# Seven short rows of matmuls behind the last product

## The chip, the cores and the metric

The kernel runs on one core of one Trainium2 chip. The metric is the device time of one execution in microseconds. Beside it stands the span of a profiled execution: the time from its first to its last instruction, as the hardware profiler recorded it.

## The reference

The reference computes two residual sublayers over a sequence of 2048 rows of 512 features, all in fp32. What matters here is the shape of the work: long products, the last of them with `w_out`.

```python
mod = (_silu(c) @ w_mod).reshape(c.shape[0], 6, 1, -1)
sa, ca, ga, sb, cb, gb = (mod[:, 0], mod[:, 1], mod[:, 2], mod[:, 3], mod[:, 4], mod[:, 5])
h = _layernorm(x) * (1 + ca) + sa
a = h @ dft_hid_re.T;  b = h @ dft_hid_im.T
x = x + ga * (dft_seq_re @ a - dft_seq_im @ b)        # Fourier mixing
h = _layernorm(x) * (1 + cb) + sb
z = gelu(h @ w_in);  z1 = z[..., :Fh];  z2 = _layernorm(z[..., Fh:])
g = w_sp @ z2 + b_sp[None, :, None]                   # gating over the sequence
x = x + gb * ((z1 * g) @ w_out)                       # the last product
```

Here S is 2048, D is 512 and Fh is 896.

## The kernel before

The kernel writes each fp32 operand as a high part, rounded to the type fp32r, and a low part, the rest. A product is then three matmuls in fp32r: high by high, high by low, low by high. The helper `matmul3` (lines 94 to 98) issues them, so nearly all matmuls of the program have its lines. `split`, `prep_hi` and `prep_lo` make the parts on ScalarE (L268) and VectorE (L286).

A matmul here has a stationary operand of 128 x 128 words, loaded into the array before it, and a moving operand of 128 partitions by 512 columns. In the profile the two are separate rows: PEld LDWEIGHTS and PE MATMUL. All moving operands of the kernel lie contiguously in SBUF. A plain fp32 product occurs once, in `keep_busy` (L368), which runs four matmuls of ones at the start while the first transfers are under way. A single fp32r matmul stands at L416.

PSUM has eight banks, and the helper `bank(k, name)` takes a tile of 128 x 512 words in bank k; a new tile under the same bank number follows the previous one there. The order of all work is written out by hand: lists of things to do at step n (`at`, `run`), in the order in which the engines then execute them.

The stages in order: the Fourier products over the sequence (tiles `gp`) and over the features (`yp`), the product with `w_in` (`fp`, `z1s`, `z1p`, `z2s`, `z2p`), the gating product over the sequence (`gw`, banks 0 to 7; its last sums are taken out on VectorE by `add_w`, L952), and the last product with `w_out` (`op`). For the last one, `make_wo` and `make_wo_lo` hold the parts of `w_out` in SBUF, seven tiles `wo_hi[f]` and seven `wo_lo[f]` of 128 x 512 words, in the profile `woh` and `wol`. `mm_o` runs 7 x 3 matmuls for each of sixteen blocks of 128 rows, with the parts of `z1 * g` (`uh`, `ul`) as the stationary operand. The outputs go to banks 4 and 5 by turns; the sixteenth goes to bank 6, into which `hold_x2` (L1032) has put the residual before. `add_o` (L1019, L1020) adds the residual of the other fifteen on VectorE and sends them out.

The last block is taken out by `halves_o`: ScalarE copies its bank to SBUF (L1039), and two transfers take the two halves, one issued from ScalarE's queue (L1041) and one from SyncE's (L1042). Line 1411 stands at the very end; the program's closing drains and semaphores carry its number in the profile.

Of the kernel before, what the change touches and what calls it, by code (L numbers as in the profile page):

```python
# [8 lines left out]
F32 = mybir.dt.float32  # L9
# [4 lines left out]
P = 128  # L14
# [5 lines left out]
def fnet_gmlp_kernel(  # L20
# [32 lines left out]
    nc = tc.nc  # L53
# [3 lines left out]
    Q = 512  # L57
# [5 lines left out]
    x = x.rearrange("b s d -> (b s) d")  # L63
# [15 lines left out]
    def bank(k, name):  # L79
        return psum.tile([P, 512], F32, tag=f"bank{k}", bufs=1, name=name)  # L80
# [814 lines left out]
    wo_hi, wo_lo, wor, Z1T = {}, {}, {}, {}  # L895
# [78 lines left out]
    def make_u(p, r, f):  # L974
        g, z = G[p, r][:, f, :], Z1T[p, r]
        if f + (0 if p in (1, 4) else 4) == NF - 1:
            nc.vector.transpose(z[:, f].rearrange("p (b i) -> p b i", i=32), z[:, 3].rearrange("p (b i) -> p b i", i=32))
        nc.vector.tensor_tensor(g, g, z[:, f, :], op=ALU.mult)
# [56 lines left out]
    def halves_o(t, i):  # L1035

        ps = OP.pop((t, i))
        o = blocks.tile([P, Q], F32, tag="t", bufs=2, name="last")
        nc.scalar.activation(o, ps, AF.Copy)  # L1039
        rows_ = slice(t * Q + i * P, t * Q + (i + 1) * P)  # L1040
        nc.scalar.dma_start(out[rows_, :D // 2], o[:, :D // 2])  # L1041
        nc.sync.dma_start(out[rows_, D // 2:], o[:, D // 2:])  # L1042

    def two_first(mm, n, k, m):

        if k % m == 0:
            mm([n, n + 1])
        elif k % m > 1:
            mm([n])
# [73 lines left out]
    for j, turn, weigh, row, fold, hi in ((0, (25, 26, 27, 28), (29, 29, 30, 30), 26, (34, 34, 35, 36), (40, 37, 38, 39)),  # L1123
# [8 lines left out]
        n = weigh[3] + 1  # L1132
# [20 lines left out]
    for t in range(NQ):  # L1153
        n = 8 * NQ * (t + 1)
        for i in range(4):
            y = N2 - 1 if t == NQ - 1 else (54, 56, 58, 60)[i] if t == 0 else n + (7, 9, 11, 13)[i] if t == 1 else n + 1 + 3 * i
# [41 lines left out]
    w0 = ctx.enter_context(ExitStack())  # L1198
# [92 lines left out]
    for i, p in enumerate(PROD):  # L1291
        for k in range(8):
            n = NB[p] + 2 * k
# [11 lines left out]
    for f in range(NF):  # L1305
        n = N4 + 24 + 8 * f
# [55 lines left out]
    for o in range(len(order)):  # L1362
# [18 lines left out]
        for q in MU.get(o, ()):  # L1381
            if q[:2] == (4, 1):
                add_bs(*q)
            make_u(*q)
    halves_o(*order[-1])
    assert not fill, fill


# [27 lines left out]
```

## Time and profile before

| | us |
|---|---|
| time, median of 2 runs | 932.57 (931.79 and 933.35) |
| span of the profiled execution | 930.9 |
| time of that execution apart from its span | not recorded |
| TensorE matmuls busy | 924.6 (99% of the span) |
| weight loads busy | 760.7 (82%) |
| VectorE busy | 737.3 (79%) |
| ScalarE busy | 409.6 (44%) |
| GpSimd busy | 198.9 (21%) |

In the rows of the profile, PE is TensorE's matmuls, PEld its weight loads, DVE VectorE, ACT ScalarE, POOL GpSimd and SP SyncE; a q behind the name is the engine's queue, that is, what it issues or waits for outside its compute work. A line of the timeline has the start and the duration in microseconds, the engine, the source line, the operation, the tiles written and read, the shape and the count, and in brackets the idle time before it with what ended that. A line of a group has the count, the busy time, the mean duration in nanoseconds, and the idle time before its instructions. A line of a source view has the shortest, median and longest duration in nanoseconds and the first and last start in microseconds. A matmul's duration reaches from its start to the end of its last result, so the durations of neighbours overlap.

### The profile page before, as it was taken

What the parts mean: (1) busy time and instruction counts of PE and PEld (TensorE: products, weight loads), DVE (VectorE), ACT (ScalarE), POOL (GpSimd) and SP (SyncE); (2) the same over time, 40 slices, a digit from 0 to 9 for tenths busy, and PEclk for the clock granted to TensorE, in tenths of its full rate; (3) what the DMA queues carried; (4) which work ended last, traced back from release to release, by engine and by line L of the source; (5) the groups of instructions that cost most, each with busy time, mean ns of one, the idle gap of its engine ahead of it and who ended that gap; (6) DMA issues with size and microseconds to landing.
All of it is one profiled execution on the core that took longest, in us unless ns stands there. A gap on an engine that the chain in (4) does not pass through costs nothing.

```text
span 930.9 us, 12343 instructions
## 1 busy us (share of the span) xinstructions
PE 924.6 (99%) x4053; PEld 760.7 (82%) x4053; DVE 737.3 (79%) x1217; ACT 409.6 (44%) x734; POOL 198.9 (21%) x376
## 2 busy tenths in 40 slices
PE   8999999999999999999999999999999999999998
PEld 5888888888888888888888888888888888888886
DVE  7789967788687677875668788899799789896762
ACT  5685424232132221322577877674544544331121
POOL 2420000224654165323512320331000000000000
PEclk9999999999999999999999999999999999999999
DMA  9995762856639977996464764444464555744651
GB/s 215 219 226 123 146 158 46 192 148 163 165 86 306 306 207 222 277 337 232 138 217 135 273 204 103 118 106 104 104 147 102 132 140 138 177 102 149 188 174 57
DMA packets 246976, 157.88 MB, mean 170 GB/s; under 512 B 140384, under 2 KB 214368, under 8 KB 246784
## 3 DMA queue, kind: packets, MB, share of 16 engines
q1 hardware_dynamic: 233248, 119.57, 52.0%
q0 software_dynamic: 12272, 36.86, 11.5%
q10 hardware_dynamic: 1392, 0.66, 0.2%
q8 instruction: 32, 0.52, 0.2%
q14 instruction: 32, 0.26, 0.1%
HBM read 120.33 MB, written 36.71 MB: 169 GB/s over the span
## 4 chain that ended last, share of the span: by engine, by line
PE 98%; DMA 1%; DVE 0%; SPq 0%; issue 0%; ACTq 0%; POOL 0%; ACT 0%; DVEq 0%
PE gp L96 12%; PE gp L97 12%; PE gp L98 12%; PE gw L97 10%; PE gw L98 10%; PE gw L96 10%; PE yp L98 3%; PE yp L96 3%; PE yp L97 3%; PE op L98 3%; PE op L97 3%; PE op L96 3%; PE fp L97 1%; PE fp L98 1%; PE fp L96 1%; PE z2s L98 1%
## 5 line engine op out<-in xcount | busy, mean ns | idle before, releaser
L268 ACT ACTIVATE ah<-t 128x512 fp32r<-128x512 f32 x236 | 149.1, 632 | 364.7 <-DVE t L189 252.5
L286 DVE TENSOR_TENSOR al<-t,ah 128x512 fp32r<-128x512 f32 x236 | 160.7, 681 | 52.6 <-PE gp L97 27.9
L97 PE MATMUL gp<-al,hh 128*128 128x512 f32 x496 | 193.0, 389 | 0.0
L96 PE MATMUL gp<-ah,hh 128*128 128x512 f32 x496 | 193.0, 389 | 0.0
L98 PE MATMUL gp<-ah,hl 128*128 128x512 f32 x496 | 192.9, 389 | 0.0
L189 DVE STREAM_TRANSPOSE t<-stage 128x512 f32<-128x512 f32 x236 | 165.7, 702 | 11.2 <-DMA stage<-in_A_dft_seq_re_dram 4.9
L97 PE MATMUL gw<-al,bh 128*128 128x512 f32 x400 | 155.6, 389 | 0.0
L98 PE MATMUL gw<-ah,bl 128*128 128x512 f32 x384 | 149.5, 389 | 0.0
L96 PE MATMUL gw<-ah,bh 128*128 128x512 f32 x384 | 149.4, 389 | 0.0
L98 PEld LDWEIGHTS gp<-ah,hl 128*128 128x128 f32 x496 | 93.1, 188 | 19.4
L96 PEld LDWEIGHTS gp<-ah,hh 128*128 128x128 f32 x496 | 93.1, 188 | 19.4
L97 PEld LDWEIGHTS gp<-al,hh 128*128 128x128 f32 x496 | 93.1, 188 | 19.4 <-DVE al L286 0.2
L97 PEld LDWEIGHTS gw<-al,bh 128*128 128x128 f32 x400 | 75.1, 188 | 15.5
L98 PEld LDWEIGHTS gw<-ah,bl 128*128 128x128 f32 x384 | 72.1, 188 | 15.5 <-DVE bl L919 0.5
L96 PEld LDWEIGHTS gw<-ah,bh 128*128 128x128 f32 x384 | 72.1, 188 | 15.0
L891 POOL DMA_DIRECT2D s_d<-sj x64 | 35.1, 548 | 106.8 <-DVE sj L883 82.4
L96 PE MATMUL yp<-hth,gh 128*128 128x512 f32 x128 | 49.8, 389 | 0.0
L97 PE MATMUL yp<-htl,gh 128*128 128x512 f32 x128 | 49.8, 389 | 0.0
L98 PE MATMUL yp<-hth,gl 128*128 128x512 f32 x128 | 49.8, 389 | 0.0
L636 POOL DMA_DIRECT2D ht_d<-hturn x62 | 41.0, 667 | 23.9 <-DVE hturn L632 18.5
L96 PE MATMUL op<-woh,uh 128*128 128x512 f32 x112 | 43.6, 389 | 0.0
L97 PE MATMUL op<-wol,uh 128*128 128x512 f32 x112 | 43.6, 389 | 0.0
(233 smaller groups left out, 1446.0 us busy)
## 6 DMA issues: line engine op xcount, KB each, us to landing
stage<-in_A_dft_seq_im_dram SPq DMA_DIRECT2D x64, 256.0 KB, 5.6
sj<-in_B_w_sp_dram SPq DMA_DIRECT2D x32, 512.0 KB, 6.8
s_d<-sj POOLq DMA_DIRECT2D x64, 256.0 KB, 4.2
stage<-s_d SPq DMA_DIRECT2D x128, 128.0 KB, 2.8
stage<-in_A_dft_seq_re_dram SPq DMA_DIRECT2D x60, 256.0 KB, 5.4
stage<-in_B_w_sp_dram SPq DMA_DIRECT2D x88, 128.0 KB, 2.9
wm<-in_w_mod_dram SPq DMA_DIRECT2D x16, 256.0 KB, 6.1
xr<-in_A_x_dram POOLq DMA_DIRECT2D x16, 256.0 KB, 4.5
```

The costliest lines, as they stand in the source:

```text
L96: nc.tensor.matmul(acc, ah, bh, start=first, stop=False, skip_group_check=go_on)
L97: nc.tensor.matmul(acc, ah, bl, start=False, stop=False, skip_group_check=go_on)
L98: nc.tensor.matmul(acc, al, bh, start=False, stop=last, skip_group_check=go_on)
L189: nc.vector.transpose(dst.rearrange("p (b i) -> p b i", i=32), block[:, :, 32 * k:32 * k + 32])
L268: nc.scalar.activation(AH[n], T[n], AF.Copy)
L286: nc.vector.tensor_tensor(AL[n], t, AH[n].bitcast(F32), op=ALU.subtract)
L636: eng.dma_start(v[a, i], ht[32 * a:32 * a + 32].rearrange("c (b r) -> c b r", r=32))
L891: nc.gpsimd.dma_start(s_d[m, r, g][b * P:(b + 1) * P, :], a)
```

## The change

Behind `halves_o` of the last block the changed kernel calls a new function, `shapes`. It issues seven rows of eight matmuls. The operands are parts of `w_out`: two stationary blocks of 128 columns, `w0` and `w1`, out of `wo_hi[1]`, and two moving tiles, `a = wo_hi[0]` and `b = wo_lo[0]`, taken by turns. Each matmul starts and ends its own sum. The outputs go to new tiles in bank 0, those of the last row to banks 0 and 1 by turns, and nobody reads them. The rows:

- `sfull`: the columns as they lie.
- `sturn`: every second column, first the even and then the odd ones.
- `sline`: every sixteenth column, from sixteen starting points.
- `sparts`: two halves of 256 columns, one behind the other.
- `sone`: the first column 512 times.
- `sboth`: by turns an fp32r matmul and one whose two operands are read as plain fp32.
- `srows`: contraction over the lower and the upper 64 partitions by turns.

```diff
+    def shapes():
+
+        a, b, w = wo_hi[0], wo_lo[0], wo_hi[1]
+        w0, w1 = w[:, :P], w[:, P:2 * P]
+
+        def row(name, pairs, n=8, banks=(0,), parts=None):
+            ps = [bank(k, f"{name}{k}") for k in banks]
+            for i in range(n):
+                l, r = pairs[i % len(pairs)]
+                o = ps[i % len(ps)]
+                if parts:
+                    p0 = parts * (i % (P // parts))
+                    o = o[p0:p0 + parts]
+                if len(r.shape) == 3:
+                    o = o.rearrange("p (x y) -> p x y", y=r.shape[-1])
+                nc.tensor.matmul(o, l, r, start=True, stop=True)
+
+        def mixed(t, y):
+            return t.rearrange("p (x y) -> p y x", y=y)
+
+        row("sfull", ((w0, a), (w1, b)))
+        row("sturn", ((w0, mixed(a, 2)), (w1, mixed(b, 2))))
+        row("sline", ((w0, mixed(a, 16)), (w1, mixed(b, 16))))
+        row("sparts", ((w0, a.rearrange("p (x y) -> p x y", x=2)), (w1, b.rearrange("p (x y) -> p x y", x=2))))
+        row("sone", ((w0, a[:, :1].broadcast_to((P, Q))), (w1, b[:, :1].broadcast_to((P, Q)))))
+        row("sboth", ((w0, a), (w1.bitcast(F32), b.bitcast(F32))))
+        row("srows", ((w[:64, :P], a[:64]), (w[64:, :P], b[64:])), banks=(0, 1))
...
     halves_o(*order[-1])
+    shapes()
     assert not fill, fill
```

## The prediction

> **What bounds the kernel now.** I read the page's busy shares first, then the chain that ended last, and then, because everything in this change stands behind the last product, the last microseconds of the timeline.
>
> ```profile
> span 930.9 us, 12343 instructions
> PE 924.6 (99%) x4053; PEld 760.7 (82%) x4053; DVE 737.3 (79%) x1217; ACT 409.6 (44%) x734; POOL 198.9 (21%) x376
> PE 98%; DMA 1%; DVE 0%; SPq 0%; issue 0%; ACTq 0%; POOL 0%; ACT 0%; DVEq 0%
> L97 PE MATMUL gp<-al,hh 128*128 128x512 f32 x496 | 193.0, 389 | 0.0
> ```
>
> TensorE is the kernel: 98% of the chain, and its groups sat idle for 0.0 us. Work that is put behind it adds to the time unless something later still runs. The mean of 389 ns is not what a matmul costs, since matmuls overlap. The cost is the distance from one start to the next, and the timeline's tail gives it, together with what follows the last product:
>
> ```profile
> 914.73 0.39 PE L96 MATMUL op<-woh,uh 128*128 128x512 f32 x1
> ...
> 926.52 0.19 PEld L98 LDWEIGHTS op<-woh,ul 128*128 128x128 f32 x1
> 926.75 0.39 PE L98 MATMUL op<-woh,ul 128*128 128x512 f32 x1
> 927.17 0.60 ACT L1039 ACTIVATE last<-op 128x512 f32<-128x512 f32 x1 [8.21 <-PE op L98]
> 927.79 0.33 SPq L1042 DMA_DIRECT2D out_dram<-last  x1
> 927.80 0.38 ACTq L1041 DMA_DIRECT2D out_dram<-last  x1
> ```
>
> From the start at 914.73 to the one at 926.75 there are 53 matmuls: 12.02 / 53 = **0.227 us** each, with the 0.19 us weight load of the next one hidden under it. The last product ends at 926.75 + 0.39 = 927.14. ScalarE empties the bank until 927.77, and two transfers take the tile out. What closes the program is in the rows of its last line and in the transfers' landing times (1.7 to 2.0 us after issue):
>
> ```profile
> DMA to landing us min/median/max: 1.7/1.9/2.0
> L1411 SPq DRAIN  x3: 7/7/7, 930.0 to 930.4; - x3
> L1411 PEldq DRAIN  x2: 13/2140/4267, 922.9 to 930.4; - x2
> L1411 SPq EVENT_SEMAPHORE  x11: 17/28/28, 928.2 to 930.8; - x11
> ```
>
> The last byte lands at about 927.8 + 2.0 = 929.8. SyncE drains at 930.0, and then come 0.9 us of drains and semaphores among the engines, up to 930.9. TensorE's own first drain starts at 922.9 and takes 4.267 us, so it ends at 927.2, with the last matmul. From there TensorE is free for 930.0 - 927.1 = 2.9 us. That is all the cover there is behind the last product.
>
> The page gives the profiled execution no time beside its span of 930.9 us. The two timed runs have a median of 932.57, which is 1.7 more; I add the change of the span to 932.57.
>
> **The change part by part.** It removes nothing and moves nothing. It adds 56 matmul calls on TensorE in seven rows of eight, each 512 columns wide, over operands that have lain in SBUF since long before. No other engine gets an instruction, no queue gets a DMA, and nobody reads the results. The eviction (L1039) and the two output transfers wait on the bank of the last product alone (bank 6), so they run as before beside the rows. The rows write banks 0 and 1, whose last reader is the adding of the last sequence product:
>
> ```profile
> 891.27 2.47 DVE L952 TENSOR_TENSOR g<-gw,g 128x512 f32<-128x512 f32 x4
> ```
>
> That reader is done at 893.74, 33 us earlier, so the first row's first matmul waits for nothing and starts one distance behind the last product's: 926.75 + 0.227 = 926.98.
>
> *Plain rows.* The first row reads contiguous columns in the same kind and size as every product here: 8 x 0.227 = **1.81 us**. The row "parts" describes the same 512 contiguous columns as two halves: 1.81. The row "one" reads one column 512 times. No row of the trace has that; it costs nothing at best (1.81), and I see no reason why reading one word again should be slower than reading a new one, so I take 1.81, with 3.44 (below) as its far end.
>
> *Whole words.* The row "both" alternates four fp32r matmuls with four plain fp32 ones. The kernel has four plain fp32 calls of this size, the warming loop of line 368, and they leave eight records:
>
> ```profile
> L368 PE MATMUL busyp<-busy,ones x8: 592/1061/1193, 1.5 to 6.9; 128*128 128x512 f32 x8
> 4.23 0.34 PEld L368 LDWEIGHTS busyp<-busy,ones 128*128 128x128 f32 x1 [0.52 <-issue]
> 5.08 0.34 PEld L368 LDWEIGHTS busyp<-busy,ones 128*128 128x128 f32 x1 [0.52 <-issue]
> 6.47 1.02 PE L368 MATMUL busyp<-busy,ones 128*128 128x512 f32 x2
> ```
>
> So a plain fp32 call is two records. Early on they come 0.85 us apart (4.23 to 5.08). The last two together run from 6.47 for 1.02 us, to 7.49, and the last of them, the shortest at 0.592, began at 6.90: 0.43 us apart. The weight loads of line 368 fall from 0.34 us to 0.19 over the same stretch, the 0.19 of the tail, so at the end of the kernel the faster figure holds. A plain fp32 call costs 2 x 0.43 = 0.86 us, and the row 4 x 0.227 + 4 x 0.86 = **4.35 us**. Changing kind between neighbours is in no row; it may cost nothing, or one emptying of the array each time. What an emptied array costs can be read where TensorE waited:
>
> ```profile
> 8.74 1.20 PE L520 MATMUL gp<-al,hh 128*128 128x512 f32 x4 [0.26 <-DVE al L286]
> 807.70 0.43 PE L98 MATMUL gw<-ah,bl 128*128 128x512 f32 x1
> 807.96 0.40 PE L96 MATMUL gw<-ah,bh 128*128 128x512 f32 x1
> ```
>
> Four matmuls after a stop take 1.20 us against 3 x 0.227 + 0.389 = 1.07, so 0.13 more; with the tail of the one before (0.389 - 0.227 = 0.16) that is 0.29 us for each emptying. A wait that is met as it is asked costs 0.03 (0.26 between the starts at 807.70 and 807.96). Seven changes of kind: 0 to 2.0 us. The six changes of row, each with a new tile in the same bank, could make TensorE wait for its own writes: 0 to 6 x 0.29 = 1.7 us. I take nothing for both, since TensorE runs in order and changes its accumulation bank throughout the products with no idle time to show for it.
>
> *Strided rows.* The row "turn" reads every second word, first the even and then the odd ones (8 bytes apart); the row "line" reads every sixteenth (64 bytes apart). All products here move contiguous columns, so the trace has no row for either. The low end is 0.227 a matmul. The nearest slower rows are the plain fp32 record, 0.43, where 512 columns take two turns each, and the plain fp32 call, 0.86. For "turn", two words apart, I take the low end, 1.81. For "line", the row farthest from what the kernel does, I take the next row up: 8 x 0.43 = **3.44**; its ends are 1.81 and 8 x 0.86 = 6.88. The nearest strided reads on another engine cost nothing, but they keep 32 words together, which "line" does not:
>
> ```profile
> L189 DVE STREAM_TRANSPOSE t<-stage 128x512 f32<-128x512 f32 x236 | 165.7, 702 | 11.2 <-DMA stage<-in_A_dft_seq_re_dram 4.9
> L286 DVE TENSOR_TENSOR al<-t,ah 128x512 fp32r<-128x512 f32 x236 | 160.7, 681 | 52.6 <-PE gp L97 27.9
> ```
>
> [...]
>
> *Half rows.* The last row contracts over 64 partitions, the lower and the upper half by turns, into two banks. Every product here has 128, so bounds again: one after the other, 8 x 0.227 = 1.81; two at a time, 4 x 0.227 = 0.91. Eight weight loads of 0.188 us, should they stay one behind another, take 8 x 0.188 = **1.50**, between the two, and I take that.
>
> ```profile
> L98 PEld LDWEIGHTS op<-woh,ul x19: 187/188/188, 914.3 to 926.5; 128*128 128x128 f32 x19
> ```
>
> [...]
>
> *The sum.* 1.81 x 4 (full, turn, parts, one) + 3.44 + 4.35 + 1.50 = 16.5 us. TensorE then ends at 926.98 + 16.5 + 0.16 (the tail of the last) = 943.7. The output landed at 929.8 and no longer counts. The closing, which began at 930.0, begins when TensorE's drain ends, and its 0.9 us follow: span 944.6, 13.7 more. **932.57 + 13.7 = 946.3 us**, 1.5% slower. If the cover of 2.9 us were absent, it would be 949.2.
>
> A measurement of this kernel tells about 2% from no change: that is 18.65 us, a time of 951.2.
>
> **Rivals.**
> 1. *Order costs nothing.* All strided matmuls go at 0.227: 1.63 less, 944.6. For it: TensorE's reads are the one thing in this trace that never falters (idle 0.0 in groups of 496). Against: they are always contiguous. With the half rows in pairs too it is 944.1, the low end.
> 2. *The joints cost.* The array empties at changes of row and of kind: up to 3.7 us more, 950.0; with half of it 948.1. Against: the 0.0 us idle at bank changes in the products. For: a tile whose only accesses are TensorE's, replaced in the same bank, is met nowhere else near in time.
> 3. *Several orders cost two turns.* "turn" and "one" go at 0.43 like "line": 2 x 1.63 more, 949.6; "turn" alone 947.9.
> 4. *The other side: slower by over 2%.* fp32r keeps its single pass only for contiguous columns, and "turn" and "line" fall to the plain fp32 price of 0.86: 5.07 + 3.44 = 8.5 more, 954.8. The place is those 16 matmuls. They are in my sum with 5.25 us; it decides from 5.25 + 4.9 = 10.2 us, an average of 0.63 each, about three turns a column. For it: the plain fp32 rows prove that the same words can be read at a quarter of the pace. Against: the kind of the matmul, not its order, made that price.
> 5. *It doesn't do what it says.* Matmuls into banks nobody reads are dropped on the way to the chip, or fit into the 2.9 us of cover: 932.6. For the second the rows would have to take a fifth of the sum, which the 0.227 excludes.
>
> **How the numbers follow.** The forecast (only "line" at two turns, joints free) has 0.35; rival 1 has 0.25, rival 2 0.16, rival 3 0.08, rival 4 0.12, rival 5 0.04 (0.01 of it for a chance reading below -2%). The range runs from 943.6, a little under rival 1's low end with a closing half a microsecond shorter, to 951.0, which takes in rivals 2 and 3 and leaves out rival 4 and rival 5: 0.16 outside. Slower by over 2% is rival 4 and a little of rivals 2 and 3 together, 0.14; faster 0.01; within 2% 0.85.
>
> **What would show it.** In the changed kernel's trace all lines up to the eviction keep their times, and the matmuls of the new line start at about 927.0 with no idle time before. Read by output tile: distances of 0.227 in "full", "parts" and "one"; 0.227 in "turn" and 0.43 in "line" (0.227 there is rival 1, 0.86 in both rival 4); twelve records in "both", eight of them 0.43 apart; the half rows in 0.9 to 1.8 us. Gaps of 0.3 at the first matmul of each row or between kinds are rival 2. The transfers land near 929.8 as before, and 0.9 us lie between TensorE's end and the span's end; a wait of the closing that comes late for another reason would put the whole sum off by that much.

## The result and the profile after

The changed kernel takes **949.64 us** (949.54 and 949.74), 1.0179 times the time before, with a 95% interval of 1.0163 to 1.0196: 17.1 us more, slower, and just under the 2% that tells a change from none. The forecast was 946.3, with a range of 943.6 to 951.0. The span grew from 930.9 to 947.8.

The busy shares say only that TensorE is still the whole kernel:

```profile
span 947.8 us, 12464 instructions
PE 944.4 (100%) x4113; PEld 771.7 (81%) x4113; DVE 737.3 (78%) x1217; ACT 409.6 (43%) x734; POOL 199.1 (21%) x376
```

The chain of the changed kernel, in order of time, shows where the 17 us lie. Its columns are start, duration, and engine, tile and line; one piece is one row of eight matmuls:

```profile
926.85 0.23 PE op L98
927.07 1.83 PE sfull L1059 x8
928.90 0.04 issue
928.95 3.91 PE sturn L1059 x8
932.86 0.04 issue
932.90 3.73 PE sline L1059 x8
936.63 0.04 issue
936.67 2.12 PE sparts L1059 x8
938.79 0.04 issue
938.84 2.01 PE sone L1059 x8
940.85 0.04 issue
940.89 4.66 PE sboth L1059 x12
945.54 0.04 issue
945.59 1.20 PE srows L1059 x8
```

From the end of the last product at 927.07 to the end of the last row at 946.79 it is 19.7 us, where the prediction had 16.5 between the same two ends. Two things stand out. "turn" is as slow as "line", 3.91 against the 1.81 that it was given. And between any two rows there is a short stop. The matmuls around the first one show it:

```profile
928.27 0.39 PE L1059 MATMUL sfull<-woh,woh 128*128 128x512 f32 x1
928.50 0.39 PE L1059 MATMUL sfull<-wol,woh 128*128 128x512 f32 x1
928.95 0.71 PE L1059 MATMUL sturn<-woh,woh 128*128 128x512 f32 x1
929.48 0.64 PE L1059 MATMUL sturn<-wol,woh 128*128 128x512 f32 x1
929.94 0.64 PE L1059 MATMUL sturn<-woh,woh 128*128 128x512 f32 x1
```

The last of "full" ends at 928.50 + 0.39 = 928.89, and "turn" begins 0.06 later; in between no matmul is in flight. From 929.48 on, a matmul of "turn" comes every 0.45 us, twice the distance of a contiguous one.

The closing is as it was: drains and semaphores for 1.0 us behind TensorE's end at 946.79.

### The profile page after: what moved, and what is told of

Read it like the earlier page. It is cut to its first block, busy times and chain, and to the rows that moved or that the text cites. A ratio compares the mean times of both kernels' runs of the same rounds, so it can differ in the third digit from the quotient of the medians.

```text
span 947.8 us, 12464 instructions
## 1 busy us (share of the span) xinstructions
PE 944.4 (100%) x4113; PEld 771.7 (81%) x4113; DVE 737.3 (78%) x1217; ACT 409.6 (43%) x734; POOL 199.1 (21%) x376
## 4 chain that ended last, share of the span: by engine, by line
PE 98%; DMA 1%; DVE 0%; SPq 0%; issue 0%; ACTq 0%; POOL 0%; DVEq 0%
PE gp L98 12%; PE gp L97 12%; PE gp L96 12%; PE gw L98 10%; PE gw L96 10%; PE gw L97 10%; PE yp L98 3%; PE yp L97 3%; PE yp L96 3%; PE op L98 3%; PE op L97 3%; PE op L96 3%; PE fp L97 1%; PE fp L96 1%; PE fp L98 1%; PE z2s L96 1%
## 5 line engine op out<-in xcount | busy, mean ns | idle before, releaser
L98 PE MATMUL op<-woh,ul 128*128 128x512 f32 x112 | 43.6, 389 | 0.0
```

Source lines behind the costliest of these rows:

```text
L98: nc.tensor.matmul(acc, al, bh, start=False, stop=last, skip_group_check=go_on)
```

## The experiments

The theory after the result had two parts. A stop comes because a row's new tile waits for the last write into the tile before it in the same bank. And a strided matmul is slow because of the order of its columns. The rival of the first part was that the change of order or kind empties the array; the rival of the second, that place, bank or weight loads make those rows slow.

**The cover.** The first row is kept alone.

```diff
         row("sfull", ((w0, a), (w1, b)))
-        row("sturn", ...)   # and the five rows behind it
```

> Only the first row (eight contiguous fp32r matmuls) is left. Theory (cover): TensorE ends at 926.9 + 8 x 0.227 + 0.16 = 928.9, ahead of the last output's landing and the drain at 930.0, so nothing is added: span 930.9, time 932.6 as before. Rival (what is put behind the last product adds its length): 2.0 us more, 934.6. The difference is 0.2%, so the span and the place of the closing decide, with the time beside them.

Measured: 932.26 us, ratio 0.9999 (0.9989 to 1.0008). TensorE's last matmul ends at 930.12, and SyncE's drain comes at 931.2, after the landing of the output, which was issued at 928.97 and took up to 2.0 us:

```profile
929.73 0.39 PE L1059 MATMUL sfull<-wol,woh 128*128 128x512 f32 x1
L1434 SPq DRAIN  x3: 7/7/7, 931.2 to 931.5; - x3
```

The eight matmuls, 1.8 us behind the last product, are free. This profiled execution was already 1.2 us later when the last product began its last matmul (927.92 against 926.75), so its longer span is not theirs.

**The stops: one tile, or the same kind in new tiles, or other banks.** Three kernels. The first keeps every order and kind but one tile a bank; the second keeps the new tiles but reads everything in order; the third keeps orders, kinds and new tiles but gives neighbouring rows different banks.

```diff
-            ps = [bank(k, f"{name}{k}") for k in banks]
+            for k in banks:
+                if k not in held:
+                    held[k] = bank(k, f"s{k}")
+            ps = [held[k] for k in banks]
```

> All seven rows as in the change, but every row writes the same tile of bank 0 (and one of bank 1 for the half rows) instead of a new tile each. Theory (a new tile in the same bank makes TensorE wait for its own last write): the six joints of about 0.31 us vanish, 949.6 - 1.9 = 947.7, and the first matmul of each row follows at the distance of its row. Rival (the array empties because the order or the kind of the reading changes): joints stay, 949.6.

```diff
+        row("sfull0", ((w0, a), (w1, b)))    # and so on to sfull6
-        row("sturn", ...)
```

> Seven rows of the contiguous kind, each in a new tile of bank 0. Theory (the new tile makes the joint): six joints stay although nothing about the reading changes; TensorE takes 56 x 0.227 + 6 x 0.31 + 0.16 = 14.7 us from 926.9, span 942.6, time 944.3. Rival (the change of order makes the joint): no joints, 12.9 us, time 942.5.

```diff
-        row("sturn", ((w0, mixed(a, 2)), (w1, mixed(b, 2))))
+        row("sturn", ((w0, mixed(a, 2)), (w1, mixed(b, 2))), banks=(1,))   # then 2, 3, 7, 0, and (1, 2)
```

> The seven rows of the change, each still in a new tile, but in banks 0, 1, 2, 3, 7, 0 and 1 with 2, so that no row follows the one before it in the same bank. Theory (a new tile waits for the last write into the previous tile of its bank): that write is over by then, the six joints shrink to a wait already met, 0.03 us each; 949.6 - 1.7 = 947.9, as with one tile (947.6). Rival (any new tile, or any change of bank, empties the array): 949.6.

Measured: one tile 947.64, seven contiguous rows 944.36, banks apart 947.27, each within 0.7 us of the first theory. The chain of the kernel with the contiguous rows has a stop before each row but the first, although nothing about the reading changes. Its first two rows:

```profile
926.78 1.83 PE sfull L1059 x8
928.61 0.04 issue
928.65 2.15 PE sfull L1059 x8
```

The chain of the kernel with banks apart has none of these stops, although order and kind change at each row:

```profile
927.16 1.81 PE sfull L1059 x8
928.97 3.62 PE sturn L1059 x8
932.59 3.47 PE sline L1059 x8
936.06 1.85 PE sparts L1059 x8
937.91 1.73 PE sone L1059 x8
939.64 4.35 PE sboth L1059 x12
943.99 1.13 PE srows L1059 x8
```

The kernel with one tile a bank takes the same 17.96 us in one piece:

```profile
926.65 17.96 PE s L1063 x60
```

So neither a new tile nor a new order makes these stops. A new tile in the bank just written does. The first weight load of "turn" shows the wait: in the changed kernel it starts only behind the last matmul of "full", and with banks apart it runs under that matmul, as weight loads do within a row.

```profile
928.94 0.18 PEld L1059 LDWEIGHTS sturn<-woh,woh 128*128 128x128 f32 x1 [0.48 <-PE sfull L1059]
```

```profile
928.59 0.19 PEld L1059 LDWEIGHTS sturn<-woh,woh 128*128 128x128 f32 x1
```

The rows with banks apart also give the terms without stops: 17.96 us in all, so the six stops cost 19.72 - 17.96 = 1.8 us. Set row against row, they are not alike: five cost 0.30 to 0.35 us, and the one before the half rows only 0.12. The half rows start late even with banks apart: their piece of 1.13 us is 0.2 longer than four pairs at 0.227 would be. That late start comes with the change from plain fp32 to fp32r and from 128 partitions to 64; no run separates the two.

**The order alone.** The two strided rows read their columns as they lie.

```diff
-        row("sturn", ((w0, mixed(a, 2)), (w1, mixed(b, 2))))
-        row("sline", ((w0, mixed(a, 16)), (w1, mixed(b, 16))))
+        row("sturn", ((w0, a), (w1, b)))
+        row("sline", ((w0, a), (w1, b)))
```

> As the change, but the rows of every second and of every sixteenth column read their columns as they lie. Theory (each strided matmul takes two turns a column): 8 x (0.455 - 0.227) + 8 x (0.433 - 0.227) = 3.5 us less, 949.6 - 3.5 = 946.1, joints unchanged. Rival (those rows are slow for their place in the sequence, their bank or their weight loads): about 949.6.

Measured: 945.86, 3.8 us less. The two rows fall to the length of the others, in their old places and behind the same stops:

```profile
929.28 2.15 PE sturn L1059 x8
931.43 0.04 issue
931.48 2.13 PE sline L1059 x8
```

**Which orders cost.** Four kernels with other rows in place of the seven, one timed execution each. The diffs from here on are shortened: a loop variable, three dots or a comment stand for rows that the kernels write out. The first takes every y-th word, the second keeps n neighbouring words together, the third and fourth read the bytes as plain fp32 and as bf16.

```diff
+        row(f"sy{y}", ((w0, mixed(a, y)), (w1, mixed(b, y))))                # y = 1 to 256
+        row(f"s{n}by{y}", ((w0, groups(a, y, n)), (w1, groups(b, y, n))))    # "p (x y n) -> p y x n"
+        row("pline", ((w0, mixed(a, 16)), (w1, mixed(b, 16))), 4)            # a, b, w0, w1 as plain fp32
+        row("h8", ((w0, mixed(a, 8)[:, 0:4]), (w1, mixed(b, 8)[:, 0:4])))    # all as bf16
```

> Nine rows of eight fp32r matmuls, 512 columns each, reading every y-th word, y = 1, 2, 4, 8, 16, 32, 64, 128, 256 (4 bytes to 1 KB apart), each in a new tile. Theory (two neighbouring words are read in one turn; any other next word costs a turn of its own): 0.227 us a matmul at y = 1 and 0.43 to 0.46 at all others, with no step at 16 bytes. [...]

> Rows of eight fp32r matmuls whose columns jump but keep n neighbouring words together: n = 2 (jumps of 16, 64 and 256 bytes), n = 4 (jumps of 32, 64, 256 bytes), n = 8 and n = 16 (jumps of 256 bytes). Theory (a pair of neighbouring words is one turn): 0.22 to 0.24 us a matmul in all of them, however far the jumps. Rival (four words, a 16-byte line, are the unit): n = 2 at 0.43 or so, n = 4 and above at 0.23. Rival (any jump breaks the run): all between 0.25 and 0.45, falling with n.

> Four rows of four plain fp32 calls (two records each): contiguous, every second, every sixteenth, one word 512 times. Theory (the reading gives one word a turn, and plain fp32 takes two turns a column anyway): all rows at 0.43 us a record, the stride hidden. Rival (a strided column doubles whatever the matmul took): 0.86 a record in the two strided rows.

> Rows of eight bf16 matmuls of 512 columns on the same bytes read as half words: contiguous, every second half word (4 bytes apart), every fourth (8 bytes), every eighth (16 bytes), one 512 times. The numbers mean nothing. Theory (two reads in the same 8 bytes make one turn): 0.22 for contiguous, every second and one; 0.43 for every fourth and eighth. Rival (only exact neighbours are free): 0.43 from every second on. Rival (a line of 16 bytes is the unit): 0.22 up to every fourth, 0.43 at every eighth.

The distances between starts, as means over the last five of a row:

```
fp32r, every y-th word   y = 1 .227   2 .451   4 .461   8 .431   16 .433   32 .434   64 .553   128 .283   256 .216
fp32r, n words together  n = 2, jumps 16/64/256 B: .453 .431 .487    n = 4, jumps 32/64/256 B: .232 .225 .277
                         n = 8, jumps 256 B: .253                    n = 16, jumps 256 B: .240
plain fp32, per record   in order .429   every second .450   every sixteenth .858   one word .430
bf16                     in order .216   every 2nd .226   every 4th .452   every 8th .900
```

These misses were of use. The theory of pairs (two neighbouring words a turn) is refuted: two together cost 0.43 to 0.49. Its rival of four words came out for jumps of up to 64 bytes and missed at 256. Single words far apart missed their 0.43 to 0.46 as well, with 0.553 at y = 64, 0.283 at 128 and 0.216 at 256. "Strides are hidden under plain fp32" held only for every second word. For bf16 none of the three expectations came out. But much the same price runs through plain fp32 and bf16, if it is counted by pieces of 16 bytes, called lines from here on. That size is an estimate from these rows: the bf16 distance doubles as the half words move from 4 to 8 to 16 bytes apart (0.226, 0.452, 0.900), plain fp32 pays no more for 64 bytes (0.858), and with jumps of up to 64 bytes four fp32r words together took 0.225 and 0.232 where two took 0.431 and 0.453. Every eighth half word meets a new 16-byte line at each of 512 columns, 0.900 / 512 = 1.76 ns a line; every fourth meets 256 lines, 0.452 / 256 = 1.77; every second 128, 0.226 / 128 = 1.77; plain fp32 at every sixteenth word 0.858 / 512 = 1.68. No row of the table went below 0.216 (0.43 a record for plain fp32), also where its lines would take less: contiguous bf16 meets 64, at 1.77 ns 0.113, and took 0.216.

fp32r fits this price in a sketch: its even and odd columns are read as two streams, each keeping its line. Every second word: each stream meets 256 lines, 256 x 1.77 = 0.453, and 0.451 was measured. Contiguous: 128 lines, 0.227, so by this sketch even the kernel's own products were bound by their lines, above the 0.216. And every 256th word, the strangest number of the table, fits: the columns alternate between the two halves of the tile, each stream runs contiguously through its half, 64 lines, and the 0.216 is left. The price is not quite one number: it is 1.80 ns a line at y = 4 and 1.69 at y = 8 to 32. And the fast row at y = 256 could also have been a matter of far jumps, so:

**Two streams.**

```diff
+        row("zfar", ...)     # "p (y x) -> p x y", y=2: words 0, 256, 1, 257, ...
+        row("zfour", ...)    # "p (x y n) -> p x n y", y=2, n=4: words 0, 4, 1, 5, 2, 6, 3, 7, 8, ...
+        row("zeight", ...)   # n=8            +  ztwo: n=2, words 0, 2, 1, 3, ...
+        row("zlines", ...)   # y=4, n=4: words 0, 4, 8, 12, 1, ...
+        row("ztwice", ...)   # words 0, 0, 1, 1, ...
+        row("zload", ...)    # weights 8 bytes apart, columns in order   +  zsame: in order
```

> Eight rows of eight fp32r matmuls, written in order into a new tile each. Theory (two streams: even and odd columns are read apart, each keeps the 16-byte line that it read last, and a new line costs a stream 1.7 to 1.78 ns): every second column from the other half of the tile (far): 64 lines a stream, so the 0.216 us that 512 columns need at least, less than the 0.227 of contiguous columns; two neighbouring lines zipped word by word (four), and eight words by eight (eight): 0.216; the words 0, 2, 1, 3 of each line (two): both streams meet all 128 lines, 0.227; four lines zipped (lines): each stream changes between two lines at every column, 0.43 to 0.46; each word twice (twice): 0.216; contiguous columns with weights read 8 bytes apart (load): 0.227 if the load stays hidden; contiguous (same): 0.227. Rival (one stream that wants four neighbouring words, and far jumps escape it by a second bank): far 0.216, but four and eight 0.43 to 0.46, two 0.43, twice 0.43.

Measured, again as distances: far 0.216, four 0.216, eight 0.216, two 0.232, lines 0.269, twice 0.216, load 0.233, same 0.229. The chain's pieces, without the stops:

```profile
926.22 1.74 PE zfar L1063 x8
...
928.00 2.01 PE zfour L1063 x8
...
930.05 2.01 PE zeight L1063 x8
...
932.11 2.12 PE ztwo L1063 x8
...
934.27 2.42 PE zlines L1063 x8
...
936.74 2.01 PE ztwice L1063 x8
...
940.99 2.10 PE zsame L1063 x8
```

"four" jumps only 16 bytes and is as fast as "far", which the rival excluded. Seven of eight rows came within 0.006 us of what two streams want. "lines" did not: a stream that changes between two lines at each of its columns should have paid 0.43 to 0.46 and paid 0.269. Nor does the sketch give 0.283 at y = 128 or the excess of jumps of 256 bytes (0.553 at y = 64, 0.487 for pairs of words). So two streams are a sketch that most rows bear out, not a shown mechanism: how many lines a stream keeps, and what far jumps add, stays open. What the runs show without it is that "far", "four" and "eight" run the same words at 0.216, where contiguous ones took 0.229 in the same kernel ("same").

**A faster kernel.** The streams say that all contiguous fp32r products here lose 0.227 - 0.216 = 0.011 us each. Two kernels without the seven rows read the moving tiles by turns from their two halves; what empties a bank puts the columns back in order. In the diff, shortened and with two small helpers written in place, `halves` is the view "p (y x) -> p y x" of a tile in SBUF and `unturned` the view "p (x y) -> p y x" of its bank.

```diff
+    def matmul3_t(acc, ah, al, bh, bl, *a):
+        matmul3(acc.rearrange("p (x y) -> p x y", y=2), ah, al,
+                bh.rearrange("p (y x) -> p x y", y=2), bl.rearrange("p (y x) -> p x y", y=2), *a)
...
-            matmul3(GW[r, f], ...)
+            matmul3_t(GW[r, f], ...)
...
-        nc.vector.tensor_tensor(g[:, f, :], GW[r, f], g[:, f, :], op=ALU.add)
+        nc.vector.tensor_tensor(halves(g[:, f, :]), unturned(GW[r, f]), halves(g[:, f, :]), op=ALU.add)
```

> The kernel before, without the seven rows, in which 3456 of its matmuls (the products into gp, gw, yp and op) read their moving columns by turns from the two halves of the tile; what empties the banks puts the columns back in order, so that nothing is left out. Two streams: each of these matmuls takes 0.216 instead of 0.227 us where TensorE isn't kept waiting, 3456 x 0.0107 = 37 us less, 932.6 - 37 = 896; VectorE (79% busy) and the reordering reads of PSUM may take some of it back, up to 905. Rival (in the long run something else holds the distance at 0.227, the weight loads or the words' supply): 932 as before.

> As by_turns, but only the products into gp and gw (2736 matmuls) read by turns; yp and op (720) read in order. Theory (each matmul so read gains 0.0107 us, and by_turns lost some 6 us of its 37 to operands that came late in gp): 901.5 + 720 x 0.0107 = 909.2. Rival (the gain came from one stage, or from a different course of the whole): 901 or 932 according to the stage.

Measured: 901.50 us with 3456 matmuls by turns, ratio **0.9671** (0.9655 to 0.9687), and 909.62 with 2736 of them, ratio 0.9754 (0.9721 to 0.9787). The gain grows with the count, as expected: 30.7 us against 23.0, each from the kernel before beside it, 7.7 us for 720 more. The second figure is rough, since its four times lie between 907.5 and 913.4. Windows of 100 us show the pace. The columns are stretch, length, then busy time and count by engine; first the kernel before, then two stretches of the one with 3456:

```profile
220.00:320.00 100.00, 100.00 (x443) 82.81 (x442) 76.72 (x123) 26.61 (x44) 49.69 (x76) 1.00 0.76 209
```

```profile
20.00:120.00 100.00, 97.67 (x452) 84.63 (x451) 89.66 (x157) 59.99 (x123) 20.43 (x60) 1.00 0.92 177
220.00:320.00 100.00, 100.00 (x465) 87.58 (x464) 76.96 (x127) 27.09 (x46) 50.13 (x78) 1.00 0.77 216
```

465 matmuls run where 443 did. Early on it is 452, with TensorE idle for 2.3 us: some of the missing 6 us (37 expected, 31 gained) went to operands that came late. The chain shares of this kernel say the same, PE is no longer 98%:

```profile
PE 80%; DVE 9%; DMA 6%; issue 2%; SPq 1%; ACT 1%; POOL 0%; ACTq 0%; DVEq 0%; POOLq 0%
```

## Why the prediction was right, point by point

The sign held and the time lies in the range, but the single forecast, 946.3, was 3.3 us low. "turn" and the stops between rows had been taken at nothing, 1.8 us each, and the half rows 0.4 too dear. The range held because it took in rivals 2 and 3, which priced the first two. That rival 3 as a whole gives 949.6, the time itself, is chance: half of its price stood on "one", which was free, and the stops made up for it.

- *Start and cover.* Forecast 926.98, found 926.91 for the first matmul. That a short row would be free was shown by the cover kernel.
- *Plain rows.* 1.81 each; without stops 1.81 ("full"), 1.85 ("parts") and 1.73 ("one"). Reading one word again was faster, which fits the sketch: it meets one line only.
- *"turn".* This step failed: 1.81 was chosen, 3.62 measured, 1.8 us of the miss. Rival 3 had it at 3.44, nearly what it cost. That words 8 bytes apart come as fast as neighbours was the author's estimate, which no run shows: in the run of strides a matmul of every second word came every 0.451 us, a contiguous one every 0.227.
- *"line".* 3.44 taken, 3.47 measured. The size was right by luck: it was given to "line" for lying farthest from what the kernel does, and "turn", next to it, costs as much.
- *Whole words.* 4.35 taken, 4.35 measured: the eight records of L368 were the right rows, and changing kind within the row is free.
- *Half rows.* 1.50 was taken as the loads' bound, and 1.13 was measured without the stop. They run in pairs, which would be 0.91; the rest is the late start, part of it between the first pair and the second, 0.34 us apart where later pairs are 0.23. The starts of a pair lie 0.01 us apart or less. These lines are from the kernel with banks apart:

```profile
943.92 0.50 PE L1059 MATMUL srows<-woh,woh 64*128 64x512 f32 x1
943.92 0.50 PE L1059 MATMUL srows<-wol,woh 64*128 64x512 f32 x1
944.26 0.39 PE L1059 MATMUL srows<-woh,woh 64*128 64x512 f32 x1
944.26 0.39 PE L1059 MATMUL srows<-wol,woh 64*128 64x512 f32 x1
944.49 0.39 PE L1059 MATMUL srows<-woh,woh 64*128 64x512 f32 x1
```

- *Joints.* Nothing was taken; six stops cost 1.8 us, five of them 0.30 to 0.35 each. The prediction's prices from the early waits, 0.29 for an emptying and 0.03 for a wait, add up to that. Rival 2 had the mechanism for the changes of row, not for the changes of kind within "both". The reason given against it, that the products change banks without a stop, was a true row read wrongly: they change to a bank whose last write lies further back, in the last product a block of 21 matmuls, 21 x 0.227 = 4.8 us.
- *Sum.* 16.5 + 1.8 ("turn") + 1.8 (stops) - 0.4 (half rows) = 19.7, as measured.
- Of the rivals, part of 2 and part of 3 happened together; 4 did not, since no fp32r row came near 0.86.

## What to carry to other kernels

The distance between matmul starts (0.227 us here), not their duration (0.39), shows what binds them; 0.227 where 0.216 is possible is a loss that a 99% busy TensorE hides. In fp32r, moving columns taken by turns from two contiguous halves were cheaper than contiguous ones (0.216 against 0.227), and every second word up to every 64th cost about double or more (0.43 to 0.55). Rotate banks rather than put a new tile into the bank just written: that cost 0.30 to 0.35 us before five rows here and 0.12 before the half rows.

## What had not been expected of the hardware

In the bf16 kernel, the row of every eighth half word kept its 0.90 us while the granted clock fell from 1.00 to 0.50, so that clock did not set its pace. The one-word row behind it ran at 0.43, twice the 0.216 that contiguous bf16 columns took at full clock:

```profile
936.00:938.00 2.00, 2.00 (x4) 0.28 (x3) 0.00 (x0) 0.00 (x0) 0.00 (x0) 1.00 0.00 0
940.00:941.70 1.70, 1.70 (x2) 0.13 (x1) 0.00 (x0) 0.00 (x0) 0.00 (x0) 0.50 0.00 0
941.79:945.30 3.51, 3.51 (x8) 0.99 (x7) 0.00 (x0) 0.00 (x0) 0.00 (x0) 0.51 0.00 0
```

The clock is the first of the last three numbers: 1.00, 0.50, 0.51, with matmuls in flight all the time. Why it fell, no run shows. Also, VectorE and ScalarE took no longer in the kernel by turns, where they read PSUM at every second word. The 32 subtractions of L92 on VectorE take 688 ns on average in the kernel before (first line) and in the kernel by turns (second), and ScalarE's 32 copies of L91 597 and 595 ns.

```profile
L92 DVE TENSOR_TENSOR gl<-gp,gh 128x512 fp32r<-128x512 f32 x32 | 21.2, 688 | 6.0 <-ACT gh L91 6.0
```

```profile
L92 DVE TENSOR_TENSOR gl<-gp,gh 128x512 fp32r<-128x512 f32 x32 | 20.5, 688 | 5.7 <-ACT gh L91 5.7
```
